# Tap bands first on GpSimd, fewer filler matmuls ahead of the first conv, and unit 1 through DRAM in place of TensorE transposes

## The chip, the cores and the metric

One Trainium2 chip, one of its cores. The metric is device time in microseconds. The kernel before took 818.68 us (median of 3 runs, 817.69 to 819.22). A run of this kernel varies by about 1 us either way.

## The reference, cut to what matters

```python
# a causal depthwise conv, then a gated feed-forward block
# x [8, 4096, 192], weight [8 heads, 7 taps]; moe_w_gate, moe_w_val [192, 1536]; moe_w_out [1536, 192]
w = softmax(weight, axis=-1)                      # (with 1e-9 in the denominator)
y[b, s, h, :] = sum_k w[h, k] * x_padded[b, s + k, h, :]      # 24 channels to a head
g = y @ moe_w_gate
out = (g * sigmoid(g) * (y @ moe_w_val)) @ moe_w_out          # 32768 tokens, float32
```

## The kernel before

Tokens go in 64 blocks of 512; two blocks make a unit, so there are 32 units. A unit's conv is a banded (Toeplitz) matmul with its result in `stage`, tokens on partitions. The feed-forward matmuls want channels on partitions (`xq`), so each block is transposed: either on TensorE (30 small transposes into PSUM, then copies), or through DRAM: written out, read back by three DMA transposes (the hop). A slot is one step of the main loop: a gate group of three matmuls for chunk g, a val group for chunk g-1, then the output matmuls. A unit has 24 slots. Each unit's conv is computed during the unit before it. The filter matrix of the conv, `toep`, is made in the head: VectorE compares an index tile (`diag`, from an iota) with each tap's number, copies the taps through these masks into `band`, and the `tps` matmuls spread the bands into the matrix. Fillers are matmuls whose result nobody uses; they are there to keep TensorE active, for the sake of its clock.

The head, before the loop (cut):

```python
wraw = const_pool.tile([1, H * K], fp32, ...)
nc.sync.dma_start(out=wraw, in_=...)              # the taps
first = fetches(0)
while first:
    emit_fetch(first)                             # three x loads, issued by GpSimd
# [cut]
nc.tensor.matmul(wbc, ones, wraw, start=True, stop=True)
emit_busy(11)                                     # filler matmuls 128x128 by 384, results unused
# [cut]
diag = const_pool.tile([NB, BG], i32, ...)
nc.gpsimd.iota(diag, pattern=[[-1, BG]], base=0, channel_multiplier=1)
nc.gpsimd.affine_select(out=shift, ...)
emit_gv_load(0)                                   # weight loads, issued by GpSimd
# [cut]
for k in range(K):
    nc.vector.tensor_scalar(masks[k], diag, scalar1=k, scalar2=None, op0=ALU.is_equal)
# [cut: softmax of the taps on VectorE and ScalarE: wmax, wexp, wsum, wn]
for k in range(K):
    nc.vector.copy_predicated(band, masks[k]..., wn[:, :, k : k + 1]...)
for b in range(G // BG):
    nc.tensor.matmul(tps[:, b], shift[:, b]..., band, start=True, stop=True)
emit_busy(17)
nc.scalar.copy(hi, tv)                            # the filter matrix toep = hi + lo
nc.vector.tensor_tensor(lo, tv, hi, op=ALU.subtract)
for fill in range(2):
    emit_conv(0, fill, spare=(fill == 1))         # conv of unit 0
    emit_relay()                                  # a GpSimd nop between matmuls that swap banks
    # [cut: copies to stage]
emit_wo_load(1)
first = fetches(1)                                # x of unit 1
while first:
    emit_fetch(first)
emit_busy(5)
for b in range(UB):
    emit_pe_transpose_out(b, emit_pe_transpose(b))    # both blocks of unit 0 on TensorE
emit_busy(4)
```

In the loop (cut), `s` is the slot in unit `u`:

```python
gate = ppool.tile(...)                            # 2 PSUM buffers each for gate and val
val = ppool.tile(...)
emit_gv(gate, val)
c0 = 13 if u == 0 else 1                          # conv of unit u+1 at slots c0 and c0+3
sil[g] = emit_silu(gate[0])                       # ScalarE
# [cut: output matmuls, conv of unit u+1]
emit_h(sil.pop(g - 1), val[0], hlists[vb])        # VectorE: h = sig * val, frees the val buffer
f0 = 14 if u == 0 else 0                          # x of unit u+2 fetched from slot f0
d0 = c0 + 4
if u == 0:
    if s == d0:
        emit_to_dram(UB + 1)                      # second block of unit 1: through DRAM
    if s == d0 + 1:
        emit_pe_transpose_out(UB, emit_pe_transpose(UB))   # first block: on TensorE
else:
    if s == d0:
        emit_to_dram((u + 1) * UB)
    if d0 < s <= d0 + NQ:
        emit_transpose((u + 1) * UB, s - d0 - 1)  # three DMA transposes, issued by SyncE
    if s == d0 + NQ:
        emit_to_dram((u + 1) * UB + 1)
```

## Time and profile before

| what | before |
|---|---|
| median | 818.68 us |
| span of the profiled run | 816.75 us |
| first conv matmul | 15.23 us |
| first gate matmul (slot 0) | 19.07 us |
| slot 0 to slot 24 (unit 0) | 25.05 us |
| slot 24 to the start of unit 31 (30 units) | 742.80 us |
| the rest | 29.83 us |

The lower rows are read from the starts of matmuls in the trace and add up to the span. For slot 24 and for unit 31 the mark is the second pair of gate and val matmuls, some 0.2 us after the first. From first gate matmul to first gate matmul, unit 0 takes 24.82 us. The page, its first part (busy time, share, instructions) and its chain of waits:

```profile
span 816.7 us, 30960 instructions
...
PE 807.5 (99%) x12925; PEld 512.0 (63%) x12925; DVE 558.6 (68%) x863; ACT 554.8 (68%) x967; POOL 134.2 (16%) x196
...
PE 98%; DVE 1%; POOL 0%; issue 0%; ACT 0%; POOLq 0%
```

TensorE (PE) is busy for all of the span that matters, and the chain that ended last lies on it. Time can come only from the head, from what TensorE does that the result does not need, or from waits.

The timeline of the kernel before, the lines of the head and of the transposes in unit 0, then a few at slot 24 and near 160 us. The columns are start, duration (of all instructions of a merged line), engine, source line, operation, output<-inputs, sizes, count, and in brackets the idle time before with what ended it:

```profile
3.58 0.20 POOL L165 IOTA diag<- 19x13 int32 x1
...
3.81 0.62 DVE L192 TENSOR_SCALAR mask_140<-diag 19x13 int32<-19x13 int32 x1 [1.45 <-POOL diag L165]
...
4.80 0.21 DVE L198 TENSOR_REDUCE wmax<-wbc 19x8 f32<-19x56 f32 x1
...
8.37 0.27 DVE L216 COPY_PREDICATED band<-mask_152,wn 19x104 f32<-19x104 int32 x1
...
8.78 2.00 PE L226 MATMUL tps<-band,shift 19*128 19x104 f32 x8 [2.60 <-DVE band L216]
...
10.72 4.58 PE L154 MATMUL busy<-idle 128*128 128x384 f16 x17
...
11.36 0.59 DVE L236 TENSOR_TENSOR toep<-tps,toep 128x416 f16<-128x416 f32 x1 [2.72 <-ACT toep L235]
...
15.23 0.24 PE L283 MATMUL cps_198<-x_0_82,toep 58*64 58x120 f16 x1
...
16.54 0.99 PE L154 MATMUL busy<-idle 128*128 128x384 f16 x5
...
38.38 0.19 PE L341 MATMUL gate<-identity,stage 52*128 52x52 f16 x1
...
38.76 0.38 PE L365 MATMUL gate<-xq,w_sb 64*128 64x512 f16 x1
...
38.95 0.81 ACT L353 COPY xq<-gate 128x780 f16<-128x780 f16 x1 [0.27 <-PE val L341]
...
39.36 0.37 PE L365 MATMUL val<-xq,w_sb 64*128 64x512 f16 x1
...
39.81 0.37 PE L365 MATMUL gate<-xq,w_sb 64*128 64x512 f16 x1
...
44.10 0.38 PE L365 MATMUL gate<-xq,w_sb 64*128 64x512 f16 x1
...
44.31 0.38 PE L365 MATMUL gate<-xq,w_sb 64*128 64x512 f16 x1
...
159.85 0.69 DVE L380 TENSOR_TENSOR h<-sig,val 128x512 f16<-128x512 f16 x1 [0.46 <-PE val L365]
...
160.69 0.38 PE L365 MATMUL gate<-xq,w_sb 64*128 64x512 f16 x1
160.70 0.38 PE L365 MATMUL val<-xq,w_sb 64*128 64x512 f16 x1
```

Two things stand there. The masks wait 1.45 us for an iota that stands behind three DMA issues on GpSimd, and the 17 fillers run until 15.3 us although the filter matrix is complete at 11.36 + 0.59 = 11.95. And in unit 0 the transposes of one block take TensorE 0.38 us, and the PSUM tile they occupy delays a gate group from 39.41 to 39.81.

The clock column needs care. The fillers are spaced 0.32 us until 13.89 us and 0.16 to 0.17 after, so TensorE ran at half rate until then. The profile's clock says 1.00 for that stretch, because the trace's clock records begin with the first change: in this run with one that says full, at 14.10 us.

### The profile page before, as it was taken

What the parts mean: (1) busy time and instruction counts of PE and PEld (TensorE: products, weight loads), DVE (VectorE), ACT (ScalarE), POOL (GpSimd) and SP (SyncE); (2) the same over time, 40 slices, a digit from 0 to 9 for tenths busy, and PEclk for the clock granted to TensorE, in tenths of its full rate; (3) what the DMA queues carried; (4) which work ended last, traced back from release to release, by engine and by line L of the source; (5) the groups of instructions that cost most, each with busy time, mean ns of one, the idle gap of its engine ahead of it and who ended that gap; (6) DMA issues with size and microseconds to landing.
All of it is one profiled execution on the core that took longest, in us unless ns stands there. A gap on an engine that the chain in (4) does not pass through costs nothing.

```text
span 816.7 us, 30960 instructions
## 1 busy us (share of the span) xinstructions
PE 807.5 (99%) x12925; PEld 512.0 (63%) x12925; DVE 558.6 (68%) x863; ACT 554.8 (68%) x967; POOL 134.2 (16%) x196
## 2 busy tenths in 40 slices
PE   7999999999999999999999999999999999999997
PEld 4666666666666666666666666666666666666665
DVE  4666667666667667767666676667677677676675
ACT  3767766767667767667676666777667676677664
POOL 6112111111111111102111111111111121011100
PEclk9999999999999999999999999999999999999999
DMA  7575545556557455456565455555466554455431
GB/s 102 74 130 103 102 99 124 101 109 115 91 105 130 91 112 113 90 116 113 108 108 100 101 120 104 116 105 90 107 118 113 114 101 92 112 123 98 87 79 41
DMA packets 185594, 84.89 MB, mean 104 GB/s; under 512 B 146020, under 2 KB 180413, under 8 KB 185453
## 3 DMA queue, kind: packets, MB, share of 16 engines
q0 software_dynamic: 52048, 42.26, 29.6%
q1 hardware_dynamic: 133132, 40.45, 23.9%
q8 instruction: 101, 1.65, 0.8%
q14 instruction: 41, 0.33, 0.1%
q10 hardware_dynamic: 272, 0.20, 0.1%
HBM read 34.95 MB, written 41.41 MB: 93 GB/s over the span
## 4 chain that ended last, share of the span: by engine, by line
PE 98%; DVE 1%; POOL 0%; issue 0%; ACT 0%; POOLq 0%
PE gate L365 60%; PE val L365 2%; PE busy L154 1%; PE acc_419 L393 0%; PE acc_420 L393 0%; PE tps L226 0%; PE acc_18207 L393 0%; PE acc_13400 L393 0%; PE acc_4995 L393 0%; PE acc_19063 L393 0%; PE acc_18540 L393 0%; PE acc_14603 L393 0%; PE acc_14338 L393 0%; PE acc_11936 L393 0%; PE acc_10999 L393 0%; PE acc_5330 L393 0%
## 5 line engine op out<-in xcount | busy, mean ns | idle before, releaser
L380 DVE TENSOR_TENSOR h<-sig,val 128x512 f16<-128x512 f16 x768 | 520.4, 688 | 243.0 <-PE val L365 240.5
L375 ACT ACTIVATE sig<-gate 128x512 f16<-128x512 f32 x768 | 458.5, 597 | 242.3 <-PE val L365 210.1
L365 PE MATMUL val<-xq,w_sb 64*128 64x512 f16 x2304 | 590.4, 376 | 0.0
L365 PE MATMUL gate<-xq,w_sb 64*128 64x512 f16 x2304 | 590.1, 376 | 0.1
L393 PEld LDWEIGHTS <-h 64*128 64x128 f16 x6120 | 269.2, 94 | 119.6
L365 PEld LDWEIGHTS <-w_sb 64*128 64x128 f16 x4608 | 214.0, 94 | 143.5 <-issue 1.7
L427 POOL DMA_DIRECT2D out_dram<-o_sb x63 | 48.5, 770 | 414.2 <-PE val L365 376.4
L283 PEld LDWEIGHTS <-toep 58*64 58x64 f16 x2048 | 29.4, 106 | 26.9 <-issue 13.5
L113 POOL DMA_DIRECT2D x_0_82<-in_x_dram x40 | 28.3, 708 | 71.2 <-PE val L365 58.5
L113 POOL DMA_DIRECT2D x_1_83<-in_x_dram x33 | 23.9, 724 | 94.2 <-PE val L365 80.5
L307 POOL COPY stage<-stage 128x640 f16<-128x640 f16 x32 | 23.0, 720 | 46.3 <-ACT sig L375 37.5
L154 PE MATMUL busy<-idle 128*128 128x384 f16 x37 | 10.1, 442 | 0.0
L98 POOL MEMSET x_0_82<- 6x192 f16 x8 | 2.0, 248 | 39.6 <-PE acc_1390 L393 5.8
L154 PEld LDWEIGHTS <-idle 128*128 128x128 f16 x37 | 4.3, 126 | 4.4 <-issue 3.6
L393 PE MATMUL acc_2929<-wo_sb,h 64*128 64x192 f16 x48 | 5.2, 243 | 0.0
L393 PE MATMUL acc_12537<-wo_sb,h 64*128 64x192 f16 x48 | 5.2, 243 | 0.0
L393 PE MATMUL acc_1993<-wo_sb,h 64*128 64x192 f16 x48 | 5.2, 243 | 0.0
L393 PE MATMUL acc_3793<-wo_sb,h 64*128 64x192 f16 x48 | 5.2, 243 | 0.0
L393 PE MATMUL acc_4731<-wo_sb,h 64*128 64x192 f16 x48 | 5.2, 243 | 0.0
L393 PE MATMUL acc_5330<-wo_sb,h 64*128 64x192 f16 x48 | 5.2, 243 | 0.0
L393 PE MATMUL acc_5595<-wo_sb,h 64*128 64x192 f16 x48 | 5.2, 243 | 0.0
L393 PE MATMUL acc_6533<-wo_sb,h 64*128 64x192 f16 x48 | 5.2, 243 | 0.0
(561 smaller groups left out, 879.2 us busy)
## 6 DMA issues: line engine op xcount, KB each, us to landing
out_dram<-o_sb POOLq DMA_DIRECT2D x63, 384.0 KB, 3.4
x_1_83<-in_x_dram POOLq DMA_DIRECT2D x31, 240.0 KB, 4.9
x_0_82<-in_x_dram POOLq DMA_DIRECT2D x24, 240.0 KB, 4.2
x_0_82<-in_x_dram POOLq DMA_DIRECT2D x8, 216.0 KB, 3.6
w_sb<-in_moe_w_gate_dram POOLq DMA_DIRECT2D x3, 192.0 KB, 4.9
wo_sb<-in_moe_w_out_dram POOLq DMA_DIRECT2D x2, 288.0 KB, 5.3
w_sb<-in_moe_w_val_dram POOLq DMA_DIRECT2D x3, 128.0 KB, 4.9
xc_769<-stage SPq DMA_DIRECT2D x2, 130.0 KB
```

Source lines behind the costliest of these rows:

```text
L98: nc.gpsimd.memset(x16[0:pad, 0, :], 0.0)
L113: nc.gpsimd.dma_start(out=dst, in_=src)
L154: nc.tensor.matmul(busy, idle[:, 0:P], idle[:, 0 : UB * D], start=True, stop=True)
L283: mm = nc.tensor.matmul(conv["ps"][a][i * Q : (i + 1) * Q, :, e, :], toep[a * Q : a * Q + R, h, c, :], x16[a * Q : a * Q + R, i * CG : (i ...
L307: nc.gpsimd.tensor_copy(conv[u][:, :, :, D:XD], conv[u][:, :, :, 0:Q])
L365: last_mm[0] = nc.tensor.matmul(ps, w_r[lo : lo + Q, q, ts(j, P)], xq[lo : lo + Q, q, :], start=(q == 0), stop=(q == NQ - 1),)
L375: nc.scalar.activation(sj, ps, AF.Silu)
L380: nc.vector.tensor_tensor(hj, sj, ps, op=ALU.mult)
L393: mm = nc.tensor.matmul(acc[a][:, i, :], hlist[j][lo : lo + Q, ts(2 * a + i, P)], wo_r[lo : lo + Q, j, :], start=(j == 0 and half == 0 and ...
L427: return lambda: nc.gpsimd.dma_start(out=o_v, in_=o_sb)
```

## The change

Its intent: issue the iota that the tap bands need ahead of the x loads; cut fillers that only hold up the first conv (11 fewer ahead of it, one more after it); let unit 1 take the path through DRAM that all later units take, so that TensorE does 30 transposes less, with its conv moved from slot 13 to slot 7 to give that path time.

```diff
--- before.py
+++ after.py
@@ -120,6 +120,8 @@
     nc.sync.dma_start(
         out=wraw, in_=bass.AP(tensor=weight.tensor, offset=0, ap=[[H * K, 1], [1, H * K]])
     )
+    diag = const_pool.tile([NB, BG], i32, tag="diag", name="diag")
+    nc.gpsimd.iota(diag, pattern=[[-1, BG]], base=0, channel_multiplier=1)
     first = fetches(0)
     while first:
         emit_fetch(first)
@@ -161,8 +163,6 @@
     nc.scalar.activation(warm, idle[:, 0:1], AF.Exp)
 
 
-    diag = const_pool.tile([NB, BG], i32, tag="diag", name="diag")
-    nc.gpsimd.iota(diag, pattern=[[-1, BG]], base=0, channel_multiplier=1)
 
     shift = const_pool.tile([NB, G // BG, 2, Q], fp32, tag="shift", name="shift")
     nc.vector.memset(shift, 0.0)
@@ -226,7 +226,7 @@
         nc.tensor.matmul(
             tps[:, b], shift[:, b].rearrange("p a r -> p (a r)"), band, start=True, stop=True
         )
-    emit_busy(17)
+    emit_busy(6)
 
     tv = tps.rearrange("p b h d -> p h b d")
     hi, lo = (
@@ -437,7 +437,7 @@
     first = fetches(1) if n_units > 1 else []
     while first:
         emit_fetch(first)
-    emit_busy(5)
+    emit_busy(6)
     for b in range(UB):
         emit_pe_transpose_out(b, emit_pe_transpose(b))
     emit_busy(4)
@@ -460,7 +460,7 @@
             hlists.setdefault(vb, [])
         emit_gv(gate, val)
 
-        c0 = 13 if u == 0 else 1
+        c0 = 7 if u == 0 else 1
         if more and s - c0 in (1, 4):
             emit_conv_out(u + 1, (s - c0) // 3, 0)
         if live:
@@ -504,23 +504,14 @@
                     emit_fetch(todo)
 
             d0 = c0 + 4
-            if u == 0:
-                if s == d0:
-                    emit_to_dram(UB + 1)
-                if s == d0 + 1:
-                    emit_pe_transpose_out(UB, emit_pe_transpose(UB))
-            else:
-                if s == d0:
-                    emit_to_dram((u + 1) * UB)
-                if d0 < s <= d0 + NQ:
-                    emit_transpose((u + 1) * UB, s - d0 - 1)
-                if s == d0 + NQ:
-                    emit_to_dram((u + 1) * UB + 1)
-
-        if u == 1 and live and s < NQ:
-            emit_transpose(UB + 1, s)
-        if more and u > 0 and 18 <= s < 18 + NQ:
-            emit_transpose((u + 1) * UB + 1, s - 18)
+            if s == d0:
+                emit_to_dram((u + 1) * UB)
+            if d0 < s <= d0 + NQ:
+                emit_transpose((u + 1) * UB, s - d0 - 1)
+            if s == d0 + NQ:
+                emit_to_dram((u + 1) * UB + 1)
+            if 18 <= s < 18 + NQ:
+                emit_transpose((u + 1) * UB + 1, s - 18)
         if s % NCH == 5 and stores or not live:
             for st in stores:
                 st()
```

## The prediction

> **What bounds it now.** TensorE: 99% busy on the page; the chain of waits is 98% PE. From unit 1 on, the first conv matmuls of successive units start at 45.8, 70.5, 95.3 us (view of the x tiles): 24.75 us a unit, gapless. Units 1 to 31 are left alone. Only the head (to 19.1 us, the first gate matmul) and unit 0 (19.1 to 43.9) can give time.
>
> **The head, from the timeline.** GpSimd issues three x loads (1.31 to 3.52), then the iota (3.58, 0.20). VectorE, idle since 2.36, waits 1.45 us for it. The first mask takes 0.62 us, until the GpSimd select ends (4.41); the maximum follows at 4.80, the band ends at 8.64. Then tps matmuls (8.78 to 10.78), 17 fillers to 15.3, conv at 15.23. The filter matrix is ready at 11.95, x lands near 7.7 (issue to landing 4.9): fillers alone hold conv 3.3 us.
>
> **Costs.**
> 1. Iota first: x loads issue 0.2 us later, with slack. Masks start near 2.4. I keep the 3.84 us from maximum to band, and allow 0.2 to 0.5 us for the select meeting a later VectorE step. Band ends near 7.4: -1.2 us, all on the chain.
> 2. Fillers 17 to 6. They are spaced 0.32 us until 13.89 us, 0.17 after. The Trainium skill ("TensorE: Matmul & The Clock Gate", Part 1) says half rate until about one 3.4 us window of sustained activity, free-running; the trace agrees. Six cold ones take 1.9 us against 4.5: -2.6 us. The matrix is ready 1.2 us after tps, so they cover it. Conv near 11.3.
> 3. Cost of that: conv, filler and transposes may run at half clock until between 10.6 and 14 us. All of it cold I estimate at 2 to 2.4 us; expected +0.6. One more filler after conv: +0.17.
> 4. Unit 1's first block through DRAM removes 30 transposes and their copies from unit 0. There the transposes start at 38.38, the next gate group at 38.76, the one after waits until 39.81 instead of 39.41, because ACT's copy (0.81 us) holds the PSUM tile: -0.75 us on PE. The hop (write, landing, three transposes) takes about 8 us in later units (75.4 to 83.1). Written at slot 11, 11 to 12 us after the first gate matmul, it is ready some 4 us before slot 24. No wait expected.
> 5. Conv of unit 1 moves from slot 13 to 7. Its x landed near 24.2, 5.1 us after the first gate matmul; slot 7 is about 7.2 us after: 2 us spare. The last weights land near 15.5, wanted after 16: no wait.
>
> **Sum.** -1.2 -2.6 +0.6 +0.2 -0.75 = -3.8 us, practically all on the critical path. Predicted **814.8 us**, range **812.6 to 816.9** (8 in 10). Faster by over 2%: 0.01; within 2%: 0.98; slower: 0.01.
>
> **What would show each step.** Masks at 2.4 instead of 3.8, band end at 7.1 to 7.7. First conv at 10.6 to 11.6. First gate matmul near 16 (15 to 17). In unit 0 the transposes shrink from 90 to 60 matmuls, and first gate matmul to the second unit's start is 24.0 us instead of 24.8. Later units still 24.75. SyncE's queue shows two hops for unit 1, the first ending 3 us or more before use.
>
> **What would make it wrong.** The clock staying low well past the first conv, so cold matmuls eat the gain (816 or above). PE waiting at slot 7 for x, or early for weights, since loads get less lead. Masks slowed by GpSimd's DMA issue. The hop late at slot 24. Better than predicted if activity from 7.5 us on releases the clock before conv: then 813.

## The result, and the profile after

| what | before | after | difference |
|---|---|---|---|
| median, runs of one set | 818.18 (4 runs) | 816.44 (815.59 to 816.88, 4 runs) | -1.74 |
| span of the profiled run | 816.75 | 813.81 | -2.94 |
| first conv matmul | 15.23 | 9.22 | -6.01 |
| first gate matmul | 19.07 | 14.64 | -4.43 |
| slot 0 to 24 | 25.05 | 24.67 | -0.38 |
| slot 24 to unit 31 | 742.80 | 744.49 | +1.69 |
| the rest | 29.83 | 30.01 | +0.18 |

The ratio is 0.9976 (95% interval 0.9959 to 0.9993). Such a ratio is the mean time of one kernel's runs over that of the other's of the same rounds, so it is not quite the ratio of the medians quoted. All outputs are right. The profiled run was the quickest of its four. The first gate matmul comes 4.43 us sooner, more than I predicted, and then 1.69 us are lost again in units that the change does not touch.

The page after, and below it a line from the waits of TensorE's weight loads between 45 and 800 us (engine and line, what was waited for: total us, times, longest):

```profile
span 813.8 us, 30886 instructions
...
PE 805.9 (99%) x12885; PEld 516.9 (64%) x12885; DVE 557.9 (69%) x862; ACT 554.4 (68%) x966; POOL 134.4 (17%) x196
...
PE 97%; POOL 1%; DMA 1%; issue 0%; DVE 0%; POOLq 0%
```

```profile
PEld L365 <- issue: 1.9, 6, 0.4
```

In the kernel before the line of the waits is missing in the same stretch. The timeline after, the lines that answer to those above, then two waits in unit 0, then one of the six places:

```profile
0.85 0.13 POOL L124 IOTA diag<- 19x13 int32 x1 [0.39 <-POOLq L533]
...
2.29 0.10 DVE L192 TENSOR_SCALAR mask_140<-diag 19x13 int32<-19x13 int32 x1
...
6.67 0.27 DVE L216 COPY_PREDICATED band<-mask_152,wn 19x104 f32<-19x104 int32 x1
...
7.08 1.10 PE L226 MATMUL tps<-band,shift 19*128 19x104 f32 x8 [1.13 <-DVE band L216]
...
8.12 1.17 PE L156 MATMUL busy<-idle 128*128 128x384 f16 x6
...
8.76 0.59 DVE L236 TENSOR_TENSOR toep<-tps,toep 128x416 f16<-128x416 f32 x1 [1.82 <-ACT toep L235]
...
9.22 0.31 PE L283 MATMUL cps_187<-x_0_82,toep 58*64 58x120 f16 x1
...
11.41 1.68 PE L156 MATMUL busy<-idle 128*128 128x384 f16 x6
...
14.64 0.60 PE L365 MATMUL gate<-xq,w_sb 64*128 64x512 f16 x2
...
22.08 0.21 PE L283 MATMUL cps_463<-x_1_83,toep 58*64 58x120 f16 x1 [0.18 <-DMA x_1_83<-in_x_dram]
...
39.30 0.38 PE L365 MATMUL gate<-xq,w_sb 64*128 64x512 f16 x1
...
39.66 0.37 PE L365 MATMUL gate<-xq,w_sb 64*128 64x512 f16 x1
...
155.56 0.69 DVE L380 TENSOR_TENSOR h<-sig,val 128x512 f16<-128x512 f16 x1 [0.81 <-PE acc_3490 L393]
...
156.04 0.38 PE L365 MATMUL gate<-xq,w_sb 64*128 64x512 f16 x1
...
156.30 0.37 PE L365 MATMUL val<-xq,w_sb 64*128 64x512 f16 x1
...
156.30 0.31 PEld L365 LDWEIGHTS <-w_sb 64*128 64x128 f16 x4 [0.38 <-issue]
```

What to read there:

- The masks start at 2.29 instead of 3.81 us. The tps matmuls take 1.10 us instead of 2.00: the clock was full at that moment. But the first conv's matmuls take 0.31 us instead of 0.24, and the fillers after it 1.68 us for six instead of 0.99 for five: half rate again.
- At 22.08 the conv of unit 1 waits for its x, and at slot 24 two gate matmuls stand 0.36 us apart instead of 0.22: the last DMA transpose came just then.
- At 156.04 gate and val, which should start together, fall 0.26 us apart. The multiply h on VectorE began late at 155.56 (idle 0.81 us, where 0.46 is usual), so the val buffer came free late. There are six such breaks, and the difference to the kernel before shrinks by about 0.25 us at each: from -4.65 at slot 25 to -3.12 at the last gate groups.

So three questions: what makes the breaks, what the clock does in the head, and what the hop costs.

### The profile page after: what moved, and what is told of

It is laid out like the page before. It is cut to its first block, busy times and chain, and to the rows that moved or that the text cites. A ratio compares the mean times of both kernels' runs of the same rounds, so it can differ in the third digit from the quotient of the medians.

```text
span 813.8 us, 30886 instructions
## 1 busy us (share of the span) xinstructions
PE 805.9 (99%) x12885; PEld 516.9 (64%) x12885; DVE 557.9 (69%) x862; ACT 554.4 (68%) x966; POOL 134.4 (17%) x196
## 4 chain that ended last, share of the span: by engine, by line
PE 97%; POOL 1%; DMA 1%; issue 0%; DVE 0%; POOLq 0%
PE gate L365 57%; PE val L365 5%; DMA x_1_83<-in_x_dram 1%; PE acc_15500 L393 0%; PE acc_6494 L393 0%; PE acc_10960 L393 0%; PE acc_6758 L393 0%; PE acc_752 L393 0%; PE acc_12762 L393 0%; PE acc_3754 L393 0%; PE acc_15764 L393 0%; PE acc_15765 L393 0%; PE acc_3755 L393 0%; PE acc_12763 L393 0%; PE acc_6759 L393 0%
## 5 line engine op out<-in xcount | busy, mean ns | idle before, releaser
L393 PEld LDWEIGHTS <-h 64*128 64x128 f16 x6120 | 276.3, 94 | 114.6
L365 PEld LDWEIGHTS <-w_sb 64*128 64x128 f16 x4608 | 221.3, 94 | 143.2 <-issue 3.0
L156 PE MATMUL busy<-idle 128*128 128x384 f16 x27 | 7.3, 429 | 0.0
L393 PE MATMUL acc_7095<-wo_sb,h 64*128 64x192 f16 x48 | 5.2, 243 | 0.0
L393 PE MATMUL acc_10697<-wo_sb,h 64*128 64x192 f16 x48 | 5.2, 243 | 0.0
L393 PE MATMUL acc_1089<-wo_sb,h 64*128 64x192 f16 x48 | 5.2, 243 | 0.0
L393 PE MATMUL acc_1690<-wo_sb,h 64*128 64x192 f16 x48 | 5.2, 243 | 0.0
L393 PE MATMUL acc_2291<-wo_sb,h 64*128 64x192 f16 x48 | 5.2, 243 | 0.0
L393 PE MATMUL acc_2554<-wo_sb,h 64*128 64x192 f16 x48 | 5.2, 243 | 0.0
L393 PE MATMUL acc_3155<-wo_sb,h 64*128 64x192 f16 x48 | 5.2, 243 | 0.0
L393 PE MATMUL acc_3754<-wo_sb,h 64*128 64x192 f16 x48 | 5.2, 243 | 0.0
L393 PE MATMUL acc_4093<-wo_sb,h 64*128 64x192 f16 x48 | 5.2, 243 | 0.0
```

Source lines behind the costliest of these rows:

```text
L156: nc.tensor.matmul(busy, idle[:, 0:P], idle[:, 0 : UB * D], start=True, stop=True)
L365: last_mm[0] = nc.tensor.matmul(ps, w_r[lo : lo + Q, q, ts(j, P)], xq[lo : lo + Q, q, :], start=(q == 0), stop=(q == NQ - 1),)
L393: mm = nc.tensor.matmul(acc[a][:, i, :], hlist[j][lo : lo + Q, ts(2 * a + i, P)], wo_r[lo : lo + Q, j, :], start=(j == 0 and half == 0 and ...
```

## The experiments

For the breaks I took every multiply h and compared its start with the moment at which its val group, its sigmoid and VectorE's own last instruction were done. The median is 138 ns. In the kernel before none of the 768 exceeds it by 120 ns after the first dozen slots. In the changed kernel eleven do, by 180 to 375 ns. Counting all of VectorE's records in the trace from zero, waits included, their positions are (my count, not a view of the profile):

```
after:  319  447  575  703  831  959  1087  1215  1343  1471  1599
```

They are exactly 128 records apart. VectorE's stream alternates between a record that only waits for a semaphore and the multiply. In the kernel before, the record at 319 is a wait; in the changed kernel it is the multiply, because one VectorE copy (of the removed transposes' result) is gone from the stream ahead of it. Theory A: the first instruction of every 128 comes late, and that costs time only where it is the multiply; where it is the wait, it is hidden in the waiting. (In the kernel before, the waits at these positions show no delay: each ends as long after the multiply ahead of it as in the same slot of other units, within 2 ns by the median.) Rival B: DMA traffic by chance. Rival C: any extra instruction shifts the timing and helps.

### after_again: the changed kernel once more

No edit. 

> The changed kernel, unaltered, to stand beside the others on one chip. Theory A (a VectorE instruction stream read in pieces of 128 instructions: the first instruction of each piece comes about 0.3 to 0.5 us late, and costs time only where it is the multiply h itself, not the wait ahead of it): 11 late multiplies, 61 us apart, six breaks of 0.25 us in TensorE's stream again, at the same slots; 816.4 us. Rival B (the breaks come from DMA traffic of the hop or of output stores meeting by chance): breaks at other slots than in the first profile, in another number.

Measured: 816.21 us median (813.83 to 817.72, 6 runs), ratio 0.9968. Eleven late multiplies at the same positions and six breaks at the same slots, at 155.54, 277.81, 460.19, 521.86, 644.12 and 704.48 us, each 0.5 us sooner than in the first profile, because unit 0 had no wait for x and none for the hop in this run. They follow the program, not the time. That speaks against B.

### after_dve1: one VectorE instruction more

```diff
     nc.vector.tensor_tensor(lo, tv, hi, op=ALU.subtract)
+    extra = const_pool.tile([1, 1], fp32, tag="extra", name="extra")
+    nc.vector.memset(extra, 0.0)
```

> One tiny VectorE memset (1x1) more, in a stretch where VectorE idles in the head. Theory A: every 128-piece now begins at the wait, as in the kernel before; no late multiply, no break in TensorE's gate and val stream after unit 1, and 1.5 us less: about 814.9 us. Rival B: nothing changes, 816.4 us and breaks as before.

Measured: 815.10 us median (813.27 to 815.71, 5 runs), ratio 0.9950. No late multiply, no break. Slot 24 to unit 31 took 742.80 us, as in the kernel before. Here is the same place in the timeline of this kernel:

```profile
154.90 0.69 DVE L382 TENSOR_TENSOR h<-sig,val 128x512 f16<-128x512 f16 x1 [0.46 <-PE val L367]
...
155.74 0.38 PE L367 MATMUL gate<-xq,w_sb 64*128 64x512 f16 x1
155.75 0.38 PE L367 MATMUL val<-xq,w_sb 64*128 64x512 f16 x1
```

The idle time ahead of the multiply is 0.46 us, and gate and val start together. In the same rounds the mean was 1.4 us under after_again (814.66 against 816.04), and the profiles differ by 1.54 us between slot 24 and unit 31 (742.80 against 744.34). The times alone would not settle it, since the intervals of the two ratios overlap (0.9938 to 0.9962 and 0.9953 to 0.9982).

### after_dve2: two of them

```diff
+    nc.vector.memset(extra, 0.0)
+    nc.vector.memset(extra, 0.0)
```

> Two such memsets. Theory A: the pieces begin at the multiply again, one multiply earlier than in the changed kernel; late ones return every 128 instructions, about 816.2 us. Rival C (the extra instruction helps for another reason, for instance by shifting time): as with one memset, about 814.9 us. Rival B: 816.4 us, no difference among the three.

Measured: 815.30 us median (815.18 to 817.95, 5 runs), ratio 0.9967. Thirteen late multiplies and six breaks are back, at other slots, and slot 24 to unit 31 took 744.08 us. The median looks like that of one memset, the mean (816.05) like that of none; the profile decides it, because the runs scatter with the head's clock. Rival C falls.

### before_dve1: the same memset in the kernel before

The edit is that of after_dve1. 

> The kernel before with the one memset. Theory A: late multiplies appear every 128 VectorE instructions, with several breaks of 0.25 us in TensorE's stream, so 1 to 2 us slower than the kernel before: about 819.7 us. Rivals B and C: 818.2 us, no difference.

Measured: 820.44 us median (819.05 to 820.58, 5 runs), ratio 1.0016 (1.0004 to 1.0028). Twelve late multiplies appear, again 128 records apart (191, 319, 447 and so on), with five breaks after 45 us in the weight loads' waits, and slot 24 to unit 31 takes 744.06 us instead of 742.80. So one 0.06 us memset in an idle stretch cost the kernel before over a microsecond. Theory A stands, as far as the position goes: of all 14 profiles, the nine with 1699 VectorE records have no late multiply, and the five with 1698 or 1700 have 11 to 13 (my count). A multiply and its break, in the timeline of this kernel:

```profile
280.26 1.47 DVE L382 TENSOR_TENSOR h<-sig,val 128x512 f16<-128x512 f16 x2 [0.81 <-PE acc L395]
...
280.74 0.38 PE L367 MATMUL gate<-xq,w_sb 64*128 64x512 f16 x1
...
281.00 0.37 PE L367 MATMUL val<-xq,w_sb 64*128 64x512 f16 x1
```

What stands behind it is an inference. The Trainium skill ("Runtime: NRT & Kernel Launch", Instruction fetch mechanics) says that instructions are fetched in blocks by DMA, 16 KiB being 256 instructions, and that the cost of a block's boundary is "mostly hidden". The trace has an instruction queue whose larger packets are 8 KiB, which at that rate is 128 instructions. Another instruction queue moves packets of 16 KiB, so the size is not the same for all engines. In the trace of the changed kernel (my reading of its packets) the next 8 KiB packet starts 0.67 to 1.46 us after each of the eleven late multiplies has begun, and the one before it had landed at least 2.9 us earlier. So the late multiply sits where a block ends, but no packet is seen that it waits for. That a fetch is what is late is not shown; the period of 128 and its dependence on the position are.

### iota_only

```diff
+    diag = ...; nc.gpsimd.iota(diag, ...)     # ahead of the x loads
     first = fetches(0)
```

> The kernel before with the tap bands' iota first on GpSimd and nothing else; VectorE has as many instructions as before. By the changed kernel's trace the band ends 1.7 us earlier, and all 17 fillers and what follows move with it: tps at 7.1 to 7.2 us, first conv 1.6 us or more earlier, no late multiplies; 1.6 us less than before (range 1.2 to 2.4). If the x loads, issued a little later, were what holds the first conv, nothing would come of it.

Measured: 816.11 us median (814.27 to 817.90, 6 runs), ratio 0.9970: -2.5 us by the means. In its profile the band ends at 7.06 instead of 8.64 us, the tps matmuls start 1.57 us sooner, but the first gate matmul only 0.64 us sooner (18.43): that profiled run was among the two slowest of its six (817.9), the clock became full only at 14.44 us, and the fillers, there in full number, took longer for it. The spread of 3.6 us is larger than the effect. I put it down to the moment at which the clock rises, but only the run of 817.9 has a trace. Its clock also took long to come: TensorE was busy without a pause from 7.21 us, 7.2 us before the rise.

### fill_only

```diff
-    emit_busy(17)
+    emit_busy(6)
```

> The kernel before with 6 fillers in place of 17 ahead of the first conv. My prediction: 11 fillers less, -2.6 us at conv, +0.6 for cold conv and transposes: -2.0 in the end. If the cold clock costs what the changed kernel's trace suggests (first conv to first gate matmul 4.8 to 5.4 us instead of 3.84, so 1.0 to 1.6 us): -1.0 to -1.6 us. Rival: fillers cost nothing because they pay for themselves in clock: 0.

Measured: 816.88 us median (816.55 to 817.24, 5 runs), ratio 0.9976: -2.0 us by the means. Profile: first conv 12.84 us (2.39 sooner), first conv to first gate matmul 4.24 us instead of 3.84, first gate matmul 17.08 (1.99 sooner). Here the prediction's terms hold: 2.4 saved, 0.4 paid back. VectorE's count is that of the kernel before, and there is no late multiply.

### hop_only

```diff
-        c0 = 13 if u == 0 else 1
+        c0 = 7 if u == 0 else 1
# and the hop for unit 1 as in the change; fillers and iota as in the kernel before
```

> The kernel before with only the DRAM hop for unit 1 (conv from slot 7, 30 transposes gone). One VectorE copy goes with it, so the pieces of 128 begin at a multiply: 11 late ones. -0.8 us for the transposes, +1.5 for the breaks: +0.7 us slower than before (0 to +1.2). My prediction had -0.75. No wait for x at slot 7, since here the gate matmuls start at 19 us.

Measured: 820.14 us median (819.75 to 820.48, 5 runs), ratio 1.0016 (1.0003 to 1.0029): slower, by 1.3 us by the means. Unit 0 does shrink from 25.05 to 24.26 us, so the transposes' -0.79 is there. But slot 24 to unit 31 grew by 3.04 us: 1.54 from the eleven late multiplies, and 1.50 from something I had not expected, a wait at slot 24.

### hop_dve1

The hop alone with the memset of after_dve1. 

> The same with the one VectorE memset put in, which restores the count: no late multiplies; -0.8 us against before (-0.5 to -1.1), 1.5 us less than the hop alone.

Measured: 818.62 us median (818.17 to 819.54, 5 runs), ratio 0.9999 (0.9987 to 1.0011). No late multiply, but no gain either. The timeline of this kernel at slot 24:

```profile
42.46 0.38 PE L367 MATMUL gate<-xq,w_sb 64*128 64x512 f16 x1
...
43.73 0.37 PE L367 MATMUL gate<-xq,w_sb 64*128 64x512 f16 x1 [0.89 <-DMA xq<-xc]
```

Two gate matmuls stand 1.27 us apart instead of 0.21. The third DMA transpose, issued at 35.62, had not landed until about 43.7 us: 8.1 us after issue. So the 0.79 us that TensorE gains is given back as a wait of 1.06 us. In the changed kernel the same transpose lands within 0.2 us of its use; the 4 us of spare time that I predicted do not exist.

### hop_dve1_f8

```diff
-            f0 = 14 if u == 0 else 0
+            f0 = 8 if u == 0 else 0
```

> The hop alone with the VectorE memset, and unit 2's x fetched from slot 8 of unit 0 instead of slot 14. In the run without it the hop's third transpose landed 1.06 us late for slot 24, 8.1 us after its issue, with the x loads of unit 2 and an output store under way. Theory E (the x loads in front of the hop on the same DMA engines make it late): no wait at slot 24, 1.0 us less than that run: -1.2 us against before (hop_dve1 was -0.5 by medians). Rival (the hop needs 8 us whatever else moves, or the output store alone delays it): wait of about 1 us stays.

Measured: 818.72 us median (817.13 to 819.03, 5 runs), ratio 0.9996 (0.9984 to 1.0008). In the profile the wait at slot 24 is gone and slot 24 to unit 31 is 742.80 us again, although the transposes were issued later (37.0 to 41.9 us), since the write to DRAM now meets the x loads. In the times nothing is to be seen: the two ratios do not differ. So the profile speaks for theory E and the times do not confirm it. The head hides what there may be: in this profile the first gate matmul came 0.96 us later than in that of hop_dve1 (19.16 against 18.20), with the clock full only at 14.24 us.

### after_fill15_dve1: no pause in the first stretch

```diff
-    emit_busy(11)
+    emit_busy(15)
# and the memset of after_dve1
```

> The changed kernel with the VectorE memset and 15 instead of 11 fillers in the first stretch, so TensorE has no pause of about 1.1 us ahead of the tps matmuls. Theory D (that pause, in a window of 3.4 us, takes the clock back to half for the next window, so first conv, fillers and transposes run at half clock): with it gone the clock record shows no half-clock window after the first full one, first conv to first gate matmul is 4.0 us instead of 4.7 to 5.6, time 1.0 to 1.5 us less than the same without it (815.1 in its run): about 813.8 us. Rival (the tps matmuls, or the window's phase, set it whatever the fillers do): 815.1 us, half-clock window still there.

Measured: 813.29 us median (812.89 to 816.34, 6 runs), ratio 0.9941. The mean granted clock over time, in the table by stretches (start:end, length, busy time of each engine with its count, clock, DMA share, GB/s), first of the changed kernel, then of this one:

```profile
8.00:10.00 2.00, 2.00 (x36) 1.25 (x39) 0.59 (x1) 0.51 (x1) 2.00 (x4) 0.78 1.23 196
10.00:12.00 2.00, 1.85 (x50) 1.17 (x39) 1.10 (x2) 1.05 (x2) 1.81 (x3) 0.50 1.20 159
12.00:14.00 2.00, 2.00 (x66) 1.33 (x65) 0.57 (x2) 0.49 (x2) 1.90 (x3) 0.87 1.38 179
```

```profile
8.00:10.00 2.00, 2.00 (x35) 1.23 (x38) 0.59 (x2) 0.51 (x1) 2.00 (x4) 1.00 1.24 196
10.00:12.00 2.00, 1.85 (x62) 1.11 (x50) 1.31 (x2) 1.14 (x2) 1.76 (x4) 1.00 1.28 173
12.00:14.00 2.00, 2.00 (x67) 1.31 (x67) 1.01 (x2) 1.34 (x2) 2.00 (x3) 1.00 1.37 185
```

In the changed kernel the clock is full from 5.70 to 9.11 us, half until 12.53 and full again. With the four fillers more it is full from 7.52 us on, with no way back. First conv to first gate matmul takes 4.16 us, against 5.42 in the changed kernel and 5.60 in after_dve1. Of the profiled runs with 11 first fillers, all seven that reached the full clock before 7 us fell back to half for one window of 3.41 us, and the other four reached it only near 14 us. Of the three with 15 (this one and the two below) none fell back; the pause between the last filler and the tps matmuls was 1.13 us in after_dve1, nothing in this run and the next, and 0.64 us in best2. So ten profiles agree with theory D, that the pause ahead of the tps matmuls costs the clock; it is not proven. In this run and the next the clock rose only at 7.52 and 7.21 us, after the place of the pause, so that best2, with its rise at 5.62 us, is the one like-for-like case: there a pause of 0.64 us and the tps matmuls lay in the first full window, and the clock stayed. And among the timed runs with 11 fillers, the quickest of after_again (813.83), of after_dve1 (813.27) and of iota_only (814.27) have a mean clock of 1.000, where a half-clock stretch of 3.41 us would leave at most 0.998. They have no trace, but as the quickest they seem to have risen early and not fallen back, pause or no pause. By the times, this kernel's ratio is not clear of after_dve1's (0.9927 to 0.9954 against 0.9938 to 0.9962). One of the six runs took 816.34 us all the same, at a mean granted clock of 0.997 where its others had 0.999 or 1.000, so the phase of the window still seems to matter. Unit 1's conv waited 0.27 us for its x in this profile.

### best: everything together

```diff
+    nc.vector.memset(extra, 0.0)                  # with its tile, as in after_dve1
-    emit_busy(11)
+    emit_busy(15)
-    emit_wo_load(1)
     first = fetches(1) ...                        # x of unit 1 first
+    emit_wo_load(1)
-            f0 = 14 if u == 0 else 0
+            f0 = 8 if u == 0 else 0
```

> All that the experiments point to: the changed kernel with the VectorE memset, 15 fillers first, x of unit 1 fetched ahead of the second half of the output weights, and x of unit 2 from slot 8. If the gains add up: no late multiplies, first gate matmul near 13.4 us, no wait at slots 7 and 24: 813.0 to 813.8 us, 1.4 us or more under the changed kernel with the memset and 2.5 to 3.5 us under the changed kernel. Rival (loads then collide elsewhere, for instance output weights late at slot 11 or so): 815 us.

Measured: 813.04 us median (812.52 to 813.32, 5 runs), ratio 0.9930. Unit 0 takes 24.26 us, so the wait for x at slot 7 is gone. But at slot 24 the hop is late again:

```profile
38.60 0.37 PE L367 MATMUL gate<-xq,w_sb 64*128 64x512 f16 x1 [0.39 <-DMA xq<-xc]
```

The gate matmul before it started at 37.84, so 0.55 us are lost, with unit 2's x landed at 30.58 us and an output store (32.67 to 38.20) and the write of unit 1's second block (from 35.03) the other large transfers. Theory E in its first form, x loads beside the transposes, does not explain this one. But the x loads met the write to DRAM: from its issue to the first transpose it took 5.4 us here and 5.9 in hop_dve1_f8, against 2.9 to 3.5 in the eight profiles of the hop with x from slot 14.

### best2: the same with x of unit 2 from slot 14

The edit is that of best without its last two lines. 

> The combined version with unit 2's x fetched from slot 14 again, as in the changed kernel. In the combined run the hop's last transpose still came 0.55 us late at slot 24, with unit 2's x landed long before it (30.6 us) and only an output store under way; with x from slot 14 and the same 15 fillers it was on time, but unit 1's conv waited 0.27 us for its x. If fetching x from slot 8 is what delays the hop (it holds up the write to DRAM): no wait at slot 24 nor at slot 7, first gate matmul to slot 24 in 24.26 us, slot 24 on in the undisturbed 742.8 us to unit 31, 812.5 to 812.8 us. If the hop's landing is a matter of chance with whatever shares the DMA engines: a wait of 0 to 1 us at slot 24 again, 812.8 to 813.3 us.

Measured: 812.51 us median (812.45 to 813.13, 5 runs), ratio 0.9925 (0.9912 to 0.9939): the quickest of all, 6.0 us under the kernel before by the means of the same rounds. No wait at slot 7 or 24, no late multiply, 742.80 us to unit 31. Against best it gains 0.3 us by the means, in other rounds. It agrees with the thought that the fetch from slot 8 delays the hop, but with one profile each, chance is not excluded. Its first gate matmul came at 14.09 us, later than the 13.69 of after_fill15_dve1, for a reason that shows in its timeline:

```profile
10.17 0.63 POOL L140 DMA_DIRECT2D w_sb<-in_moe_w_val_dram  x1 [0.36 <-DMA w_sb<-in_moe_w_gate_dram]
...
10.85 0.24 PE L285 MATMUL gate<-x,toep 58*64 58x120 f16 x1 [0.77 <-POOLq L252]
```

The second half of the conv waits for the relay, a nop on GpSimd, which stands in order behind weight loads that GpSimd is still issuing. With the conv at 15 us these issues were over; with the conv at 9 us they can be the next limit.

## Why the prediction was right or wrong

The time, 816.44 us, lies inside the range (812.6 to 816.9), near its upper end; the expected 814.8 was 1.6 us too low. By the medians the change is worth 1.7 us, and 2.0 and 2.7 us by the means of two sets of rounds, where I had said 3.8. That it lies inside is partly luck: in the profiled run the head gained 1.4 us more than my terms for it (-4.43 against -3.0), and 2.3 us that I had not foreseen were lost after it. The terms:

- **Iota first, -1.2 us on the band: right, a little small.** The band ended at 6.93 us (predicted 7.1 to 7.7, near 7.4), 1.7 us sooner. The allowance for the select meeting VectorE was right in kind: the step of wsum that took 0.22 us takes 0.65 us beside it.
- **Fillers, -2.6 us, conv near 11.3: too small in the profiled run.** Conv came at 9.22. The clock happened to be full from 5.70 to 9.11, so tps took 1.10 us and the six fillers 1.17 instead of 2.00 and 1.9. Alone (fill_only) the saving at conv was 2.39, as I had said.
- **Cold clock, +0.6 us: too small.** The step that failed is "conv, filler and transposes may run at half clock until between 10.6 and 14 us", taken to begin cold and warm up once. In fact the clock rose early and fell back, by theory D because of the pause ahead of tps. First conv to first gate matmul grew by 1.58 us (3.84 to 5.42), of which the one filler more explains 0.17 to 0.32, by the spacings above. Together with the point above, the head gave -4.43 us in that run, where I had -3.0. The Trainium skill ("TensorE: Matmul & The Clock Gate", Part 1) gives the window as about 3.4 us, free-running, and that an idle one brings back half rate. The traces agree on the length (3.41 us each time), but the window ahead of this fall was not idle: of its 3.41 us, TensorE paused for 1.13.
- **Transposes away, -0.75 us: right.** Unit 0 shrank by 0.79 us in hop_only and hop_dve1.
- **"Ready some 4 us before slot 24. No wait expected": wrong.** I took the 8 us of later units, whose transposes are issued some 10 us before use, so that a late landing does not show. In unit 0 the three transposes were issued in 4 us, but in the hop alone the last landed 8 us after its issue, beside x loads and an output store. The changed kernel lost 0.15 us there, the hop alone 1.06 (hop_dve1) and 1.50 (hop_only). What decides between 0 and 1.5 us stays open.
- **"2 us spare" for x of unit 1 at slot 7: wrong, by a little.** With the conv at 9 us, x of unit 1 is issued while weight loads still fill the DMA engines; the issue to landing took 8.4 us instead of 5.6. It cost 0.41 us in the profiled run (22.08 instead of 21.66), 0.27 in that of after_fill15_dve1, and nothing in the profiles of after_again and after_dve1.
- **"Units 1 to 31 are left alone", "later units still 24.75": wrong, and the largest miss.** Slot 24 to unit 31 grew by 1.69 us, of which 0.15 is the hop's wait and 1.54 the breaks. after_dve1 removes them and before_dve1 makes them, so the cause is the position of VectorE's multiplies modulo 128 records, changed by the one copy that the change removed. Nothing in the source says so; the program of the loop is the same.

The whole for the profiled runs: -4.43 (head) -0.79 (transposes) +0.41 (wait for x) +0.15 (wait for the hop) +1.54 (breaks) +0.18 (the last unit) = -2.94 us, the difference of the spans. The +0.18 in the last unit appears in all versions with the hop (30.0 against 29.8 us), with and without late multiplies; it lies after the last matmul, and I did not look for its cause. That the timed runs gained less than the profiled pair I put down to the clock's phase, without traces of the others: over the two sets the changed kernel ran from 813.83 to 817.72 us.

## What to carry to other kernels

When a kernel is bound by one engine with two buffers behind it, compare the unit times of units you did not touch: here a change of one in the instruction count of another engine shifted where its late instruction fell, and one dummy instruction put it back. Fillers held up the first conv here where they only waited, and the best times came with fillers that bridged a pause. Before you move a transfer earlier, add the lead time of everything that then shares the DMA engines and the issuing queue; a latency taken from the steady state did not hold in the head here.

## What the Trainium skill lacked or had wrong

- "Runtime: NRT & Kernel Launch", Instruction fetch mechanics, gives blocks of 256 instructions and calls the cost of a boundary mostly hidden. On VectorE multiplies that stood at every 128th record came 0.18 to 0.40 us late in five profiles, and with the wrong parity of the stream that cost the kernel 1.3 to 1.5 us of 817. No page says that the position of an instruction matters.
- "TensorE: Matmul & The Clock Gate" speaks of an idle window of 3.4 us, and advises against pauses of more than about 3 us. Here a pause of 1.13 us went before a fall: in the profiles, seven of seven early rises with 11 fillers (pauses of 1.1 to 2.8 us) fell back, none of three with 15 (0 to 0.64 us), two of which rose after the place of the pause.
- The same page calls the trace's clock events unreliable, but not that nothing is recorded ahead of the first: in the kernel before the profile reads 1.00 until 14.10 us, while the fillers' spacing of 0.32 us until 13.89 shows half rate.
- "DMA: Bandwidth & Descriptors" gives a bandwidth for DMA transposes, but no time to landing beside loads and stores on the same engines; here the last of three landed 8.1 us after its issue.
